# Top-k attention with a gated MLP on one core: the candidate search in five strided segments instead of six contiguous ones

## The chip, the cores and the metric

The kernel runs on one core of one Trainium2 chip. The metric is device time in microseconds for one launch. The engines that matter are TensorE (PE), VectorE (DVE), ScalarE (ACT) and GpSimd (POOL); each works through its own list of instructions in order, and they meet only through semaphores. DMA transfers are issued here from SyncE's queue (SP), and for some weights from POOL.

## The reference

There are 8 batches of 8 heads, 576 positions and a head size of 64. For every query the 32 largest of its 576 scores are kept, the rest are masked out, and a softmax over the kept ones weights the values. The result goes through a two-layer network with a leaky ReLU.

```python
scores = scale * np.matmul(q, k.transpose(0, 1, 3, 2))
kth = np.partition(scores, -top_k, axis=-1)[..., -top_k:-top_k + 1]   # top_k = 32
scores = np.where(scores >= kth, scores, -1000000000.0)
scores = scores - np.max(scores, axis=-1, keepdims=True)
attn = np.exp(scores)
attn = attn / (np.sum(attn, axis=-1, keepdims=True) + 1e-09)
x = np.matmul(attn, v)               # then (8, 8, 576, 64) -> (4608, 512)
h = x @ w_in                         # 512 -> 2048
g = np.maximum(h, 0.0) + alpha * np.minimum(h, 0.0)
out = g @ w_out                      # 2048 -> 512
```

Only the 32nd largest score of each row has to be known: it is the threshold of the mask.

## The kernel before

Two heads make a pair, so there are 32 pairs. The rows of a pair are cut into nine tiles of 128 queries (four for each head, and a ninth that holds the last 64 queries of both). That makes 288 tiles of 128 rows by 576 scores, in the order of the list ORDER. A main loop runs over ticks n. In each tick the loop issues, by hand-written order, one stage of several tiles on each engine: scores on PE for tile n + 1, the shift and sign on ACT for tile n, the selection on DVE for tiles n − 1 to n − 7, and in what is left, matmuls of the network for batches that are finished. The lags are LAG_S = 2 for the segment search, LAG_M = 3 for the merge and LAG_W = 7 for the mask. A calendar (put and run) places the preparation of later pairs and the products with the values at fixed ticks. Nothing reorders this list later.

How the threshold of a row is found:

- From the mean and the second moment of the row's scores, the prep steps (dve_2 to dve_6, L271 to L288) make a guess: mean + 1.6 standard deviations. It is subtracted in act_b (L337), so that b is positive for scores above the guess.
- act_s (L343) takes the sign of b and sums it, which gives the number of scores above the guess. side_of (L353, POOL) turns it into SG, which says whether the 32nd score lies above or below the guess.
- flip (L359, DVE) maps b to y by bit operations, so that the largest values of y are those nearest to the guess on the wanted side. The wanted score is then the r-th largest of y, where r follows from the count.
- seg_ops (L369, DVE) cuts the 576 values of y into segments and takes the eight largest of each with one MAX8 instruction per segment. They go into C, NSEG × 8 candidates per row.
- merge_ops (L384, L386, DVE) takes the 24 largest of the candidates in order: MAX8, then MATCH_REPLACE8, which blanks the eight just found (the profile shows a small MATCH_VALUE_LOAD ahead of it), twice over, then a third MAX8. The result is L.
- sel_eq, sel_pr and sel_sum (L397 to L407) pick the r-th of the 24 for three tiles at once, limit (L413) maps it back, mask (L433) compares b with it, and POOL multiplies the mask with the exponentials (L443). A DMA transpose brings the weights to PE for the product with the values (L494).

A segment could hold more than eight of the wanted scores. So check_group (L461) keeps the largest eighth candidate of each row's segments, and checks (L473, L474) compares it with the selected value at the end. If any row of any tile fails, final_flag (L482) sets a flag and the program goes on into general_batch, which computes everything again in a slower way.

On DVE, a tick issues the mask of one tile first, then the segment searches of another and the merge steps of a third one in turn, and then flip:

```python
for i in range(max(len(segs), len(merges), 2)):
    if i < len(segs):
        segs[i]()
    if i < len(merges):
        merges[i]()
```

So with six searches and five merge steps, one search stands behind each merge step. y has two buffers, C has two, one for each group of nine tiles, and C2, the merge's scratch, has one.

## Time and profile before

| what | value |
|---|---|
| time, median of 3 runs | 873.02 us (872.99 to 875.49) |
| the profiled execution: its own time | 873.98 us |
| the profiled execution: its span | 872.1 us |
| DVE busy | 835.1 us, 96% of the span |
| ACT busy | 790.3 us, 91% |
| PE busy | 721.9 us, 83% |
| POOL busy | 431.0 us, 49% |
| segment searches (L369, MAX8) | 1728, mean 243 ns |
| merge MAX8 (L384) | 864, mean 188 ns |

The span runs from the first to the last instruction in the profile; the execution's own time has a little more around it. A row of the groups names the line, the engine, the operation, the output and input tiles with their shapes (partitions × elements), the number of instances, the busy time and the mean duration in ns, and behind the last bar the idle time of the engine just ahead of these instructions, with what ended it. Durations of neighbours on one engine can overlap, so that the sum of durations may exceed the busy time. A row of stages gives for each stretch of time the busy us and the number of instructions of each engine, the clock granted to TensorE, the busy share of DMA and its GB/s.

### The profile page before, as it was taken

The page shows a single profiled execution, that of the slowest core. Times are in us where ns is not written, and L with a number is a line of the kernel's source. Part 1 is how long each engine was busy: PE and PEld are TensorE (multiplying, and loading weights), DVE is VectorE, ACT ScalarE, POOL GpSimd, SP SyncE. Part 2 cuts the span into 40 slices and gives each one's busy share as a digit, 9 for nine tenths or more (in the row PEclk, how much of TensorE's full clock was granted, in tenths as well). Part 3 has the DMA queues.
Part 4 walks back from the last instruction along what each step waited for, and adds up shares of the span by engine and source line. Part 5 has one row for each costly group of instructions (what it writes and reads, how often), then busy time and mean ns, then how long its engine had stood idle before and what let it go on. Part 6 is the DMA issues. An engine that isn't in the chain of part 4 may idle for free.

```text
span 872.1 us, 20608 instructions
## 1 busy us (share of the span) xinstructions
PE 721.9 (83%) x5697; PEld 428.3 (49%) x5771; DVE 835.1 (96%) x5188; ACT 790.3 (91%) x1873; POOL 431.0 (49%) x630
## 2 busy tenths in 40 slices
PE   6776688778978789787987789977897988899996
PEld 4443444334554345444454445643455554566674
DVE  4999999999999999999999999999999999999992
ACT  6999999999999999889999999989999899979861
POOL 1455545555454555545555455554554555544530
PEclk9997779899979999989998999989999999999999
DMA  7999644644665545564576445475455543535442
GB/s 161 156 178 199 131 89 90 126 91 97 135 139 107 108 102 116 100 135 95 114 154 115 98 97 116 111 136 98 92 128 121 121 103 81 106 71 100 91 96 56
DMA packets 342619, 99.37 MB, mean 114 GB/s; under 512 B 334672, under 2 KB 334944, under 8 KB 342496
## 3 DMA queue, kind: packets, MB, share of 16 engines
q1 hardware_dynamic: 340144, 95.58, 54.4%
q0 software_dynamic: 1152, 2.10, 2.0%
q8 instruction: 47, 0.77, 0.4%
q14 instruction: 76, 0.62, 0.2%
q10 hardware_dynamic: 1200, 0.30, 0.2%
HBM read 36.71 MB, written 9.44 MB: 53 GB/s over the span
## 4 chain that ended last, share of the span: by engine, by line
DVE 62%; ACT 21%; PE 12%; DMA 2%; issue 1%; POOL 1%; SPq 0%; DVEq 0%; another core or an unknown queue 0%; ACTq 0%
DVE C L369 20%; DVE y L359 9%; DVE mk L433 9%; DVE C L386 8%; DVE L L384 7%; ACT b L337 5%; ACT h L343 5%; ACT e L348 4%; PE ps L328 4%; PE pz L715 3%; PE ph L697 2%; ACT gT L703 2%; DVE P L246 2%; ACT xb L523 2%; PE pu L494 1%
## 5 line engine op out<-in xcount | busy, mean ns | idle before, releaser
L443 POOL TENSOR_TENSOR w<-mk,e 128x576 bf16<-128x576 bf16 x250 | 319.3, 1277 | 337.9 <-DVE mk L433 187.5
L369 DVE MAX8 C<-y 128x8 f32<-128x96 f32 x1728 | 419.1, 243 | 0.1
L328 PE MATMUL ps<-qkT 64*128 64x288 f32 (+1 forms) x1280 | 256.5, 474 | 35.1 <-ACT b L337 34.6
L337 ACT ACTIVATE b<-ps,NT 128x576 f32<-128x576 f32 x288 | 202.3, 761 | 3.1 <-PE ps L328 3.1
L343 ACT ACTIVATE h<-b 128x576 bf16<-128x576 f32 x288 | 202.9, 705 | 1.7
L697 PE MATMUL ph<-xT,w_in_b 128*128 128x128 bf16 (+2 forms) x997 | 150.4, 292 | 40.8 <-ACT gT L703 33.6
L328 PEld LDWEIGHTS ps<-qkT 64*128 64x128 f32 (+1 forms) x1280 | 134.3, 194 | 97.6 <-ACT b L337 59.8
L348 ACT ACTIVATE e<-b 128x1152 bf16<-128x1152 f32 (+1 forms) x158 | 174.2, 1102 | 0.0
L384 DVE MAX8 L<-C 128x8 f32<-128x48 f32 x864 | 162.6, 188 | 0.1
L359 DVE TENSOR_SCALAR y<-b,SG 128x576 int32<-128x576 int32 x288 | 147.0, 510 | 8.2 <-POOL SG L353 7.8
L433 DVE TENSOR_SCALAR mk<-b,KP 128x576 bf16<-128x576 f32 x282 | 143.6, 509 | 0.0
L715 PE MATMUL pz<-w_out_b,gT 128*128 128x512 bf16 x543 | 132.4, 380 | 1.2 <-issue 0.5
L697 PEld LDWEIGHTS <-w_in_b 128*128 128x128 bf16 x1024 | 80.4, 100 | 104.0 <-issue 79.6
L703 ACT ACTIVATE gT<-ph 128x512 bf16<-128x512 f32 x140 | 86.0, 621 | 28.1 <-PE ph L697 28.1
L386 DVE MATCH_REPLACE8 C<-L,C 128x48 f32<-128x48 f32 x576 | 108.3, 188 | 0.0
L715 PEld LDWEIGHTS <-gT 128*128 128x128 bf16 x560 | 51.6, 98 | 68.5 <-issue 14.0
L494 PE MATMUL pu<-v_bf,wT 128*128 128x65 bf16 (+1 forms) x1600 | 69.4, 198 | 14.4 <-DMA wT<-w 6.9
L494 PEld LDWEIGHTS <-wT 128*128 128x128 bf16 (+1 forms) x1600 | 65.2, 103 | 25.6 <-issue 10.2
L353 POOL TENSOR_SCALAR SG<-S_all 128x1 int32<-128x1 f32 x288 | 65.3, 227 | 18.9 <-ACT h L343 18.8
L443 POOL TENSOR_TENSOR wm<-mk,e 128x576 bf16<-128x576 bf16 x32 | 40.8, 1276 | 49.9 <-DVE mk L433 45.6
L343 ACT ACTIVATION_READ_ACCUMULATOR h<-b 128x1 f32 x288 | 62.8, 218 | 0.0
L523 ACT ACTIVATE xb<-pu,rz 128x64 bf16<-128x64 f32 x224 | 54.5, 369 | 0.0
(113 smaller groups left out, 728.1 us busy)
## 6 DMA issues: line engine op xcount, KB each, us to landing
out_dram<-o_sb SPq DMA_DIRECT2D x34, 256.0 KB, 2.3
st_q<-in_q_dram SPq DMA_DIRECT2D x64, 128.0 KB, 2.8
st_v<-in_v_dram SPq DMA_DIRECT2D x64, 128.0 KB, 2.6
kst<-in_k_dram SPq DMA_DIRECT2D x62, 128.0 KB, 2.6
w_stage<-in_moe_w_out_dram SPq DMA_DIRECT2D x16, 256.0 KB, 3.1
w_in_b<-in_moe_w_in_dram POOLq DMA_DIRECT2D x8, 256.0 KB, 6.4
wT<-w SPq DMA_TRANSPOSE x128, 3.3
st_q<-in_q_dram SPq DMA_DIRECT2D x32, 32.0 KB, 2.5
```

The lines of the kernel that those rows point to most:

```text
L328: nc.tensor.matmul(o_, l_, r_, start=True, stop=True)
L337: nc.scalar.activation(t["b"].rearrange("p (a c) -> p a c", a=2), t["ps"], AF.Identity, bias=NT0[:, p * TPP + j:p * TPP + j + 1], scale=ON ...
L343: nc.scalar.activation(h, tiles[n]["b"], AF.Sign, accum_out=S_all[:, n:n + 1])
L348: nc.scalar.activation(e, tiles[n0]["bu"], AF.Exp, scale=scl)
L359: nc.vector.tensor_scalar(t["y"].bitcast(I32), t["b"].bitcast(I32), FLIP, SG[:, n:n + 1], ALU.bitwise_xor, ALU.bitwise_xor)
L369: return [lambda g=g: nc.vector.max(out=C[:, n % TPP, g, :], in_=t["y"][:, g * SEG:(g + 1) * SEG]) for g in range(NSEG)]
L384: ops.append(lambda r=r, src=src: nc.vector.max(out=L[:, 8 * r:8 * r + 8], in_=src))
L386: ops.append(lambda r=r, src=src: nc.vector.match_replace(out=C2, in_to_replace=L[:, 8 * r:8 * r + 8], in_values=src, imm_value=NEG))
L433: nc.vector.tensor_scalar(t["mk"], t["b"], row_limit(n), None, ALU.is_ge)
L443: nc.gpsimd.tensor_tensor(dst, t["mk"], t["e"], ALU.mult)
L697: nc.tensor.matmul(hold[f][:, i, :], w_in_b[:, kk, (f + i) * 128:(f + i + 1) * 128], xT[:, kk, c0:c0 + tb], start=(kk == 0), stop=(kk == N ...
L715: nc.tensor.matmul(pz[0:m], hold["gT"][:, f, r0:r0 + m], w_out_b[:, f, :], start=False, stop=(f == NFT - 1))
```

## The change

The 576 values of y are cut into five segments instead of six. A segment is no longer a block of 96 neighbours but every fifth value: segment g holds the values g, g + 5, g + 10 and so on, 116 of them for g = 0 and 115 for the others. y is fp32, so two values of a segment lie 20 bytes apart. As NSEG also sets the shapes of C and C2, a row has 40 candidates instead of 48, which the three MAX8 and two MATCH_REPLACE8 of the merge read, and the group's check reads five eighths of each row instead of six. The number of merge instructions stays.

```diff
 S = 576
-NSEG = 6
-SEG = S // NSEG
+NSEG = 5
 KW = 24
...
         C = Cs[n // TPP]
         t = tiles[n]
-        return [lambda g=g: nc.vector.max(out=C[:, n % TPP, g, :],
-                                          in_=t["y"][:, g * SEG:(g + 1) * SEG])
+        return [lambda g=g: nc.vector.max(out=C[:, n % TPP, g, :], in_=t["y"][:, g:S:NSEG])
                 for g in range(NSEG)]
```

## The prediction

> **What bounds the kernel now.** First the busy table of the profile page, then the busy time by stage, because a share over the span says nothing of where it lies.

> ```profile
> span 872.1 us, 20608 instructions
> PE 721.9 (83%) x5697; PEld 428.3 (49%) x5771; DVE 835.1 (96%) x5188; ACT 790.3 (91%) x1873; POOL 431.0 (49%) x630
> ```

> ```profile
> core 0: us, PE busy (x) PEld busy (x) DVE busy (x) ACT busy (x) POOL busy (x), PEclk, DMA share, GB/s
> 40.00:100.00 60.00, 42.61 (x273) 26.19 (x277) 58.72 (x367) 59.46 (x135) 33.61 (x48) 0.84 0.96 179
> 200.00:300.00 100.00, 82.98 (x607) 46.82 (x616) 100.00 (x631) 95.19 (x237) 52.23 (x74) 0.93 0.57 117
> 500.00:600.00 100.00, 84.46 (x684) 49.31 (x697) 100.00 (x626) 93.61 (x227) 52.49 (x74) 0.97 0.56 113
> 760.00:800.00 40.00, 37.15 (x298) 24.60 (x301) 37.15 (x224) 33.56 (x72) 20.27 (x30) 0.92 0.48 92
> 860.00:872.10 12.10, 5.40 (x59) 4.68 (x56) 0.42 (x1) 2.44 (x5) 0.00 (x0) 0.86 0.09 28
> ```

> In the two long middle stages DVE is busy 100.00 of 100 us. It never waits there, so whatever is added to its instruction stream is added to the time one for one. ACT follows at 94 to 95%: a shorter DVE stream would run into ACT soon, a longer one has nothing to hide behind. What DVE waits for outside these stages is in the list of its waits; it is all that could absorb added work:

> ```profile
> DVE y L359 <- POOL SG L353: 7.8, 6, 3.5
> DVE o_sb L606 <- DMA out_dram<-o_sb: 6.5, 1, 6.5
> DVE P L246 <- PE pr L238: 2.7, 3, 1.9
> DVE sq L271 <- ACT M L267: 1.6, 2, 1.0
> ```

> The wait at L606 is in the tail, behind the last tile, and stays. The other three sum to 12.1 us; they are waits of the tile pipeline on ACT or PE, which have room when DVE takes longer. Part of them falls before the pipeline is full, so I let 5 us be absorbed.

> **What a tile costs on DVE.** The groups by line and shape, DVE alone:

> ```profile
> L369 DVE MAX8 C<-y 128x8 f32<-128x96 f32 x1728 | 419.1, 243 | 0.1
> L384 DVE MAX8 L<-C 128x8 f32<-128x48 f32 x864 | 162.6, 188 | 0.1
> L386 DVE MATCH_REPLACE8 C<-L,C 128x48 f32<-128x48 f32 x576 | 108.3, 188 | 0.0
> L246 DVE TENSOR_TENSOR P<-pr,qkT 128x512 bf16<-128x512 f32 x32 | 21.9, 684 | 2.8 <-PE pr L238 2.7
> L407 DVE TENSOR_REDUCE KK<-L 128x3 f32<-128x72 f32 x96 | 20.7, 216 | 0.1
> L461 DVE TENSOR_REDUCE M<-C 128x9 f32<-128x54 f32 x32 | 7.5, 235 | 0.0
> L246 DVE TENSOR_TENSOR P<-pr,qkT 128x64 bf16<-128x64 f32 x32 | 6.8, 212 | 0.0
> L281 DVE TENSOR_TENSOR t<-sq,t 128x9 f32<-128x9 f32 x32 | 5.1, 159 | 0.1
> L284 DVE TENSOR_REDUCE sq<-t 128x9 f32<-128x27 f32 x32 | 5.0, 157 | 0.1
> L271 DVE TENSOR_TENSOR sq<-M,sq 128x9 f32<-128x9 f32 x32 | 4.7, 146 | 1.6 <-ACT M L267 1.6
> ```

> These durations overlap: the next instruction starts before the one in front has ended. The timeline of one tick (start, duration) shows by how much:

> ```profile
> 403.53 0.25 DVE L369 MAX8 C<-y 128x8 f32<-128x96 f32 x1
> 403.70 0.19 DVE L384 MAX8 L<-C 128x8 f32<-128x48 f32 x1
> 403.81 0.24 DVE L369 MAX8 C<-y 128x8 f32<-128x96 f32 x1
> 403.97 0.07 DVE L386 MATCH_VALUE_LOAD C<-L,C 128x8 f32 x1
> 404.03 0.19 DVE L386 MATCH_REPLACE8 C<-L,C 128x48 f32<-128x48 f32 x1
> 404.14 0.25 DVE L369 MAX8 C<-y 128x8 f32<-128x96 f32 x1
> ...
> 405.02 0.24 DVE L369 MAX8 C<-y 128x8 f32<-128x96 f32 x1
> 405.20 0.52 DVE L359 TENSOR_SCALAR y<-b,SG 128x576 int32<-128x576 int32 x1
> ```

> A search of 0.24 to 0.25 us holds the engine for 0.16 to 0.18 us, one over 48 elements (0.19) for 0.11: about 78 ns less than the duration in each case. So the path price of an instruction is its duration less 78 ns: 243 − 78 = 165 ns for a search today, 990 ns for the six of a tile.

> **The change part by part.**

> *One search fewer, each longer, read with a step of five.* Five searches cover 116, 115, 115, 115, 115 scores, 115.2 on average, and each score lies 20 bytes behind the one before it. If they lay side by side, the price would follow from three rows on one line: 48 elements 188 ns, 72 elements 216 ns (L407), 96 elements 243 ns, that is 133 ns + 1.146 ns per element. But no long step-of-five read is in the trace. The nearest row is the reduce at L461: it reads the eighth of each eight candidates, so 54 single fp32 values, 32 bytes apart. With the fixed 133 ns it pays (235 − 133) / 54 = 1.89 ns per element, against 1.146 side by side. Its nine short rows are not the reason: L284 also has nine rows, of three neighbours, and takes 157 ns for 27 elements, 126 ns + 27 × 1.146.

> The ends: with L284's 126 ns as the fixed part the reduce pays (235 − 126) / 54 = 2.02 ns. With the slope of the two L246 forms, (684 − 212) / 448 = 1.05 ns, the reduce at L407 has 216 − 72 × 1.05 = 140 ns fixed, and L461 pays (235 − 140) / 54 = 1.76 ns; the search's own fixed part is then 243 − 96 × 1.05 = 142 ns. I take 1.89 since it rests on the rows that are fitted by one line, the search among them. A search then lasts 133 + 115.2 × 1.89 = 351 ns and holds DVE for 273; five hold it 1365 ns. That is +375 ns per tile. By the low end it is 142 + 115.2 × 1.76 = 345, held 267, five 1335: +345. By the high end 133 + 115.2 × 2.02 = 366, held 288, five 1440: +450.

> [...]

> *The merge over 40 candidates.* Three MAX8 and two MATCH_REPLACE8 lose eight elements each: 5 × 8 × 1.146 = −46 ns per tile (−42 at 1.05). The two 8-value loads stay.

> *The order.* Searches and merge steps are issued in turn, six and five of them; after, five and five. A search still stands between each merge step and the one that needs its result; the last merge MAX8 now stands last, and flip or the selection follows, which don't read it directly in most ticks. Cost zero, covered by the search in between, which becomes longer. If that cover went, a merge step would wait out the 78 ns overlap, 4 × 78 ns × 288 = 90 us, but there is no reason that it goes.

> *The group's check* reads 45 values instead of 54, 32 times: 9 × 1.89 × 32 = −0.5 us. No DMA, wait or instruction of another engine moves; the tiles C and C2 shrink.

> *The sum.* Per tile 375 − 46 = +329 ns, times 288 tiles +94.8 us; less 0.5, less 5 absorbed: +89. By the ends (345 − 42) × 288 − 5.5 = +82 and (450 − 46) × 288 − 5.5 = +111. The profiled execution took 873.98 us, 1.9 more than its span, and the median of the runs is 873.02, 1.0 below it. So 872.1 + 89 + 1.9 − 1.0 = **962 us**, between 955 and 984 by the ends. As a step of 20 bytes isn't one of 32, I widen to prices of 1.64 and 2.12 ns: 0.25 ns lower is 115.2 × 0.25 × 5 × 288 = 41 us, 0.23 higher 38 us, so 921 to 1000.

> **The rivals.**

> *The step costs nothing (faster).* A search lasts 133 + 115.2 × 1.146 = 265 ns, held 187, five 935: 935 − 990 − 46 = −101 ns per tile, −29 us of DVE work. ACT at 95% of a steady stage would stand at 98%, so a few us are lost to it: about 848 us. It decides below the point where five searches cost 990 + 46 = 1036 ns, 207 each, or (285 − 133) / 115.2 = 1.32 ns per element. Speaking for it: a search may have slack per element that a fetch hides in. Against: the plain MAX8 already follows the same line as the reduce of L407, so neither has slack, and L461 lies above by 0.74 ns per element. Chance 0.06; another 0.02 that it ends within 0.3%, about what a measurement of this kernel can tell from no change.

> *A short step costs more than that of L461.* L281 reads one operand and writes its result in steps of 12 bytes, and takes 159 ns against 146 for the plain L271: 13 / 9 = 1.4 ns more per element, 2.5 in all, though with two strided streams and on only nine elements. At 2.5 ns: 133 + 288 = 421, held 343, five 1715: (1715 − 1036) × 288 − 5.5 = +190, so 1063 us. Chance 0.09. A mild price, 1.36 to 1.6 ns, gives 878 to 914 us: chance 0.04.

> *The change doesn't do what it says: the general path runs.* The flag at L482 sends the whole batch through general_batch if in any of 36,864 rows the selected value is below the eighth candidate of a segment. Larger segments make that likelier. In a count over the reference's inputs, with the threshold formula of the prep steps in fp32 and bf16, ranks from 1 to 18 below the guess are wanted, and no segment of every fifth score holds more than 7 of a row's wanted ones; eight with the wanted value elsewhere would be needed. Rounding on the chip can shift a rank by one. If it ran: 320 tiles of 128 rows with seven passes over 576 elements, 7 × (133 − 78 + 576 × 1.146) ns = 5.0 us each, 1.6 ms on top, 2.5 ms or more. Chance 0.03.

> **How the numbers follow.** The forecast, prices of 1.6 to 2.12 ns, has 0.76. Slower by over 0.3%: 0.76 + 0.09 + 0.04 + 0.03 = 0.92; same 0.02; faster 0.06. The range 920 to 1000 holds nearly all of the 0.76 and a little of the mild case; the free step and the steep one lie outside.

> **What would show it.** In the profile of the changed kernel L368 (the search, one line up) has 1440 instances over 116 or 115 elements at about 351 ns; MAX8 and MATCH_REPLACE8 over 40 at 179 ns; the middle stages have DVE at 100 of 100 us and ACT near 86; the wait of y on SG shrinks. A search at 265 ns would make the step free; a search at 421 the steep case; DVE below 98% in the middle would mean that something else bounds. A span of milliseconds is the general path.

## The result, and the profile after

The changed kernel takes 960.68 us (median of 5 runs, 960.52 to 961.57) against 873.06 us for the kernel before: a ratio of 1.0995, 95% interval 1.0982 to 1.1009. It is 10% slower. The forecast was 962 us.

The page of the changed kernel begins with these lines (busy us, share of the span, instructions):

```profile
span 958.8 us, 20320 instructions
PE 752.7 (79%) x5697; PEld 443.2 (46%) x5771; DVE 930.0 (97%) x4900; ACT 796.7 (83%) x1873; POOL 430.2 (45%) x630
...
DVE 96%; PE 1%; ACT 1%; DMA 1%; SPq 0%; issue 0%; POOL 0%; DVEq 0%; ACTq 0%
```

DVE has 288 instructions fewer and is busy 94.9 us longer (835.1 to 930.0). The span grew by 86.7 us. The last line is the chain of work that ended last, followed back through what released each step: it is now DVE for 96% of the span. On the page of the kernel before the same line is:

```profile
DVE 62%; ACT 21%; PE 12%; DMA 2%; issue 1%; POOL 1%; SPq 0%; DVEq 0%; another core or an unknown queue 0%; ACTq 0%
```

This chain leaves DVE at every release, however short the wait, so the 62% alone do not say how much DVE waited before; that is measured below. The groups of DVE by shape show which instructions grew:

```profile
L368 DVE MAX8 C<-y 128x8 f32<-128x115 f32 x1152 | 395.6, 344 | 0.0
L382 DVE MAX8 L<-C 128x8 f32<-128x40 f32 x864 | 149.6, 173 | 0.1
...
L368 DVE MAX8 C<-y 128x8 f32<-128x116 f32 x288 | 101.2, 351 | 0.1
L384 DVE MATCH_REPLACE8 C<-L,C 128x40 f32<-128x40 f32 x576 | 99.6, 173 | 0.0
```

The timeline of the changed kernel (start, duration) gives what a search holds the engine for, from one start to the next:

```profile
405.20 0.34 DVE L368 MAX8 C<-y 128x8 f32<-128x115 f32 x1
405.47 0.06 DVE L384 MATCH_VALUE_LOAD C<-L,C 128x8 f32 x1
405.53 0.17 DVE L384 MATCH_REPLACE8 C<-L,C 128x40 f32<-128x40 f32 x1
405.63 0.34 DVE L368 MAX8 C<-y 128x8 f32<-128x115 f32 x1
405.90 0.17 DVE L382 MAX8 L<-C 128x8 f32<-128x40 f32 x1
406.00 0.34 DVE L368 MAX8 C<-y 128x8 f32<-128x115 f32 x1
```

A search of 0.34 us holds DVE for 0.27, a merge step over 40 for 0.10. Over all instances in the trace the mean from start to start is 272 ns for 115 elements and 280 for 116. Per tile that is 4 × 272 + 280 = 1368 ns where six searches took 6 × 164 = 984.

The stages, and the list of DVE's waits:

```profile
200.00:300.00 100.00, 77.91 (x553) 43.38 (x560) 100.00 (x526) 84.08 (x202) 46.61 (x67) 0.86 0.54 110
...
500.00:600.00 100.00, 80.55 (x598) 45.29 (x605) 100.00 (x529) 84.88 (x209) 46.28 (x65) 0.88 0.49 96
```

```profile
DVE y L358 <- POOL SG L352: 4.8, 2, 3.2
...
DVE sq L270 <- ACT M L266: 1.0, 1, 1.0
DVE P L245 <- PE pr L237: 0.5, 1, 0.5
```

DVE stays at 100 of 100 us in the middle; ACT falls from 94 to 95% to 84 to 85%.

### The profile page after: what moved, and what is told of

It reads as the page before. It is cut to its first block, busy times and chain, and to the rows that moved or that the text cites. A ratio compares the mean times of both kernels' runs of the same rounds, so it can differ in the third digit from the quotient of the medians.

```text
span 958.8 us, 20320 instructions
## 1 busy us (share of the span) xinstructions
PE 752.7 (79%) x5697; PEld 443.2 (46%) x5771; DVE 930.0 (97%) x4900; ACT 796.7 (83%) x1873; POOL 430.2 (45%) x630
## 4 chain that ended last, share of the span: by engine, by line
DVE 96%; PE 1%; ACT 1%; DMA 1%; SPq 0%; issue 0%; POOL 0%; DVEq 0%; ACTq 0%
DVE C L368 40%; DVE y L358 13%; DVE mk L431 13%; DVE C L384 10%; DVE L L382 9%; DVE P L245 2%; DVE L L401 1%; DVE KK L405 1%; DVE EQ L395 1%; DVE KP L411 1%; DVE M L459 0%; PE ph L581 0%; DVE t L277 0%; PE pz L601 0%; DMA kst<-in_k_dram 0%
## 5 line engine op out<-in xcount | busy, mean ns | idle before, releaser
L368 DVE MAX8 C<-y 128x8 f32<-128x115 f32 (+1 forms) x1440 | 496.7, 345 | 0.1
L327 PE MATMUL ps<-qkT 64*128 64x288 f32 (+1 forms) x1280 | 261.7, 485 | 47.0 <-ACT b L336 46.3
L695 PE MATMUL ph<-xT,w_in_b 128*128 128x128 bf16 (+2 forms) x997 | 161.0, 307 | 30.8 <-ACT gT L701 21.0
L382 DVE MAX8 L<-C 128x8 f32<-128x40 f32 x864 | 149.6, 173 | 0.1
L358 DVE TENSOR_SCALAR y<-b,SG 128x576 int32<-128x576 int32 x288 | 144.0, 500 | 4.8 <-POOL SG L352 4.8
L695 PEld LDWEIGHTS <-w_in_b 128*128 128x128 bf16 x1024 | 84.2, 105 | 100.9 <-issue 72.7
L492 PE MATMUL pu<-v_bf,wT 128*128 128x65 bf16 (+1 forms) x1600 | 76.6, 207 | 68.1 <-DVE P L245 54.0
L492 PEld LDWEIGHTS <-wT 128*128 128x128 bf16 (+1 forms) x1600 | 71.7, 110 | 82.8 <-issue 64.7
L384 DVE MATCH_REPLACE8 C<-L,C 128x40 f32<-128x40 f32 x576 | 99.6, 173 | 0.0
```

The lines of the kernel that those rows point to most:

```text
L327: nc.tensor.matmul(o_, l_, r_, start=True, stop=True)
L358: nc.vector.tensor_scalar(t["y"].bitcast(I32), t["b"].bitcast(I32), FLIP, SG[:, n:n + 1], ALU.bitwise_xor, ALU.bitwise_xor)
L368: return [lambda g=g: nc.vector.max(out=C[:, n % TPP, g, :], in_=t["y"][:, g:S:NSEG]) for g in range(NSEG)]
L382: ops.append(lambda r=r, src=src: nc.vector.max(out=L[:, 8 * r:8 * r + 8], in_=src))
L384: ops.append(lambda r=r, src=src: nc.vector.match_replace(out=C2, in_to_replace=L[:, 8 * r:8 * r + 8], in_values=src, imm_value=NEG))
L695: nc.tensor.matmul(hold[f][:, i, :], w_in_b[:, kk, (f + i) * 128:(f + i + 1) * 128], xT[:, kk, c0:c0 + tb], start=(kk == 0), stop=(kk == N ...
```

## The experiments

The theory was that the cost lies in the read: each score lies alone, and DVE pays about 0.74 ns more for each. The rivals were the length of a search, each hop of the address, and contention inside the kernel. A second question came up on the way: how much a search without this penalty would gain.

**Pairs of neighbours in place of single scores.** This keeps five segments and 40 candidates.

```diff
-        return [lambda g=g: nc.vector.max(out=C[:, n % TPP, g, :], in_=t["y"][:, g:S:NSEG])
+        return [lambda g=g: nc.vector.max(out=C[:, n % TPP, g, :], in_=t["y"].rearrange("p (u w) -> p u w", w=2)[:, g:S // 2:NSEG, :])
                 for g in range(NSEG)]
```

> Five segments as in the change, but each takes every fifth pair of neighbouring scores (58 or 57 pairs, two words side by side, then a hop of 40 bytes) in place of every fifth score. Theory (what costs is that each element lies alone): a search costs as a contiguous one, held about 187 ns against the 272 between starts after the change; 5 x 187 - 6 x 164 - 45 = -94 ns per tile of DVE work, -27 us, and with ACT at 98% a few us lost: 848 us, between 843 and 858. Rival A (each hop costs, however long the run): half as many hops, 57 x 0.74 x 5 = +211 ns per tile on top, about 900 us. Rival B (the longer search costs more, the step nothing): 961 us as after the change.

Measured: 869.68 us, ratio to before 0.9952 (0.9935 to 0.997). The groups of DVE:

```profile
L368 DVE MAX8 C<-y 128x8 f32<-128x116 f32 x864 | 229.1, 265 | 0.1
...
L368 DVE MAX8 C<-y 128x8 f32<-128x114 f32 x576 | 150.4, 261 | 0.0
```

A search of 116 scores in pairs takes 265 ns, as the line of the contiguous rows gives it (133 + 116 × 1.146 = 266). So neither the length nor the hop costs: the penalty is gone with pairs. But the time is not the expected 848 us. About 22 of the 27 us that DVE was to save did not come through; this is followed up below.

**Five segments of neighbours.** The count of the change without its step.

```diff
+CUT = (0, 120, 234, 348, 462, 576)
...
-        return [lambda g=g: nc.vector.max(out=C[:, n % TPP, g, :], in_=t["y"][:, g:S:NSEG])
+        return [lambda g=g: nc.vector.max(out=C[:, n % TPP, g, :], in_=t["y"][:, CUT[g]:CUT[g + 1]])
```

> Five segments of neighbours, 120 scores in the first and 114 in the other four: the count of the change without its step. Theory: search held about 187 ns, 848 us, as with the pairs. Rival B (length): 961 us.

Measured: 870.93 us, ratio 0.9971 (0.9952 to 0.9991). The searches of 114 take 261 ns, as in the run with pairs. Pairs cost what neighbours cost, and again the time missed 848 us.

**Six segments of every sixth score.** The step without the count.

```diff
-NSEG = 5
+NSEG = 6
```

> Six segments of every sixth score, 96 each: the step without the change of count, with 48 candidates as before. Theory: a search has 96 elements at about 0.75 ns more each, held 164 + 72 = 236 ns; 6 x 72 x 288 = +124 us, some 8 absorbed: 989 us. Rival B (length): 873 us, as before.

Measured: 987.08 us, ratio 1.1303 (1.1273 to 1.1334). A search over the same 96 elements goes from 243 to 311 ns:

```profile
L368 DVE MAX8 C<-y 128x8 f32<-128x96 f32 x1728 | 537.1, 311 | 0.1
```

The expectation of 989 us is met. The step alone costs 113 us (the kernel before took 874.11 beside it); the smaller count takes back 26 of them (987 to 961). The length is ruled out as the cause.

**The step by itself, first probe.** Behind the end of the changed kernel, over a scratch tile X, 16 MAX8 (or reduces) of each shape stand back to back:

```diff
+        for i in range(16):
+            nc.vector.max(out=Z[:, 4, i, :], in_=X[:, 0:575:5])
...
+        for i in range(16):
+            nc.vector.max(out=Z[:, 11, i, :], in_=po[:, 0:290:5, :])
```

> The changed kernel, with 16 MAX8 of each of 14 shapes, and 16 reduces of two, back to back on DVE behind its end, over a scratch tile, when the other engines have nearly ended. Time between starts for 115 elements. Theory by the reduce of the trace before: contiguous about 187 ns; every step from 2 words on about 270; pairs of 58 about 187. Rival C (lines of 16 bytes, two elements of a line in a row at full rate): step 2 about 187, steps of 4 and more about 270, step 3 between. Rival D (contention with GpSimd inside the kernel): step 5 is well below 270 here. By the 2.5 ns of the steep rival, step 24 words gives about 343. The reduce over 115 shows the same difference between step 1 and step 5 as MAX8, if it lies in the read.

The timeline of the probe, 16 instances a row (start, and length of the whole group). From top to bottom: steps of 1, 2, 3, 4, 5, 6, 8, 16 and 24 words; 48 elements at step 5; 58 pairs from an even word, from an odd word, 29 fours, each with a step of five groups; 48 neighbours; then the reduce at steps 1 and 5:

```profile
954.60 2.96 DVE L936 MAX8 Z<-X 128x8 f32<-128x115 f32 x16
957.47 2.95 DVE L938 MAX8 Z<-X 128x8 f32<-128x115 f32 x16
960.34 3.44 DVE L940 MAX8 Z<-X 128x8 f32<-128x115 f32 x16
963.69 4.25 DVE L942 MAX8 Z<-X 128x8 f32<-128x115 f32 x16
967.85 4.30 DVE L944 MAX8 Z<-X 128x8 f32<-128x115 f32 x16
972.06 4.23 DVE L946 MAX8 Z<-X 128x8 f32<-128x115 f32 x16
976.20 4.32 DVE L948 MAX8 Z<-X 128x8 f32<-128x115 f32 x16
980.42 4.10 DVE L950 MAX8 Z<-X 128x8 f32<-128x115 f32 x16
984.42 5.59 DVE L952 MAX8 Z<-X 128x8 f32<-128x115 f32 x16
989.93 2.39 DVE L954 MAX8 Z<-X 128x8 f32<-128x48 f32 x16
992.25 2.96 DVE L956 MAX8 Z<-X 128x8 f32<-128x116 f32 x16
995.13 3.54 DVE L958 MAX8 Z<-X 128x8 f32<-128x116 f32 x16
998.58 2.97 DVE L960 MAX8 Z<-X 128x8 f32<-128x116 f32 x16
1001.47 1.83 DVE L962 MAX8 Z<-X 128x8 f32<-128x48 f32 x16
1003.22 2.94 DVE L964 TENSOR_REDUCE Z<-X 128x1 f32<-128x115 f32 x16
1006.08 4.29 DVE L967 TENSOR_REDUCE Z<-X 128x1 f32<-128x115 f32 x16
```

The distance of two rows over 16 is the time between starts. Neighbours take (957.47 − 954.60) / 16 = 179 ns, and a step of two words takes the same 179. A step of three takes 209, of four 260, of five 263, of eight 264, of 24 words 344. So an element that lies alone is not what costs: with a step of two each lies alone, and nothing is lost. That part of the theory falls, and rival C, lines of 16 bytes, fits: a step of two leaves two elements in each line, a step of four one. Contention is ruled out as a large part: 263 ns here against 272 in the kernel. The trace of the changed kernel says the same: searches of 115 that run wholly beside an instruction of POOL hold DVE for 273 ns (567 of them), those without one for 275 (106). The reduce has 179 and, by the length of its group, 263 as well, so the price lies in the read, not in MAX8.

**Lines of 16 bytes, second probe.** The same with other shapes.

```diff
+        X8 = X.rearrange("p (u w) -> p u w", w=8)
...
+            nc.vector.max(out=Z[:, 5, i, :], in_=X8[:, 0:58, 3:5])
...
+            nc.vector.max(out=Z[:, 6, i, :], in_=X8[:, 0:58, 0:3:2])
```

> The changed kernel with 16 MAX8 of each of 15 shapes over 116 elements behind its end, in this order: contiguous; step 2 from word 0; step 2 from word 1; 58 pairs, one in each 32 bytes, at words 0-1, 1-2, 3-4, then words 0 and 2, 0 and 4; single elements at steps of 5, 8, 12, 24, 32, 40, 48 words. Theory now (what costs is that an element is the only one taken from its 16 bytes, words 0 to 3 of an aligned four): contiguous, both steps of 2, and pairs at 0-1, 1-2 and 0 and 2 about 180 ns between starts; pairs at 3-4 and at 0 and 4, and steps of 5, 8, 12 about 263. Rival (words must be neighbours in 8 aligned bytes): 1-2 and 0 and 2 about 263. For the long steps: 24 words 344 as seen; if this goes by the step's size 32 to 48 are as much, if by a bank some are back at 263.

The rows of the pairs at words 1-2, at 3-4, at 0 and 2, at 0 and 4, and the one behind them for its start:

```profile
968.26 2.97 DVE L942 MAX8 Z<-X 128x8 f32<-128x116 f32 x16
971.14 4.28 DVE L944 MAX8 Z<-X 128x8 f32<-128x116 f32 x16
975.34 2.98 DVE L946 MAX8 Z<-X 128x8 f32<-128x116 f32 x16
978.22 4.28 DVE L948 MAX8 Z<-X 128x8 f32<-128x116 f32 x16
982.41 4.36 DVE L950 MAX8 Z<-X 128x8 f32<-128x116 f32 x16
```

Words 1-2 take 180 ns and so do words 0 and 2, which are no neighbours. Words 3-4, which are neighbours but lie in two aligned fours (counted from the start of the row), take 262, as do 0 and 4. With words 1-2 and 0 and 2 at 180 ns the rival of neighbours in 8 aligned bytes falls, which had 263 for them. In these two probes, then, an element cost more where it was the only one that the instruction took from its aligned 16 bytes before it went on: 250 to 267 ns for 115 or 116 elements, all alone, at steps of 4 to 16 words and in the pairs at 3-4 and at 0 and 4, against 179 to 181 ns where two or four came from each. This reading is rough where lone elements and pairs alternate: at a step of three half of the elements are alone, which would give 221 ns, and the first probe has 209. For the long steps the same view gave 346 ns at 24 words, 253 at 32, 283 at 40 and 253 at 48: the extra at 24 does not grow with the step, and what sets it stays open.

**Where the gain of a free read goes.** Five searches without the penalty leave DVE about 100 ns less per tile (between tiles 48 and 240, summed from start to start, searches and merge take 1653 ns before and 1566 with pairs, and 16 of these are waits), but a tile takes 2.82 us in place of 2.87, half of that. A wait is counted here, and below, where the distance to the next start is over 15 ns above the median of the same instruction. First the question whether DVE bounds at all any more:

```diff
-NSEG = 5
+NSEG = 4
```

on top of the pairs, so that DVE has yet less to do.

> The full kernel with four segments of every fourth pair, 144 scores each, 32 candidates: per tile 4 searches of about 216 ns in place of 5 of 186, and a merge over 32: some 100 ns less DVE work again. Theory (ACT with its waits on PE is the bound once DVE has less to do): no more than 3 us below the five segments of pairs, 866 to 870 us. Rival (DVE still bounds): 28 us below, about 842. If a row had more candidates in one segment than the eight kept, the general path would run, and the time would be milliseconds.

Measured: 869.27 us (0.9926 to 0.9965 of before), within half a microsecond of the run with five, as the theory had it. But the trace shows that this is no test of it, since DVE did not get less to do: searches and merge take 1586 ns per tile, 20 more than with five. Four searches cannot stand between five merge steps, and the last two merge steps follow each other directly:

```profile
406.31 0.17 DVE L384 MATCH_REPLACE8 C<-L,C 128x32 f32<-128x32 f32 x1
406.40 0.29 DVE L368 MAX8 C<-y 128x8 f32<-128x144 f32 x1
...
406.98 0.17 DVE L384 MATCH_REPLACE8 C<-L,C 128x32 f32<-128x32 f32 x1
407.19 0.20 DVE L382 MAX8 L<-C 128x8 f32<-128x32 f32 x1
```

With a search behind it a MATCH_REPLACE8 takes 93 ns to the next start, with the MAX8 that reads its result right behind it 211 (189 of each). This is the cover whose loss the prediction priced at 78 ns; here it costs 118.

What holds the five segments of pairs is better read from their own trace. Its stages:

```profile
200.00:300.00 100.00, 83.78 (x638) 46.36 (x639) 99.76 (x606) 96.62 (x240) 52.80 (x75) 0.95 0.59 118
...
500.00:600.00 100.00, 85.56 (x702) 49.24 (x702) 99.75 (x604) 96.19 (x234) 53.81 (x77) 0.98 0.59 115
```

DVE's 99.75 us look as full as before, but the busy share does not show waits that are shorter than the overlap of durations (78 ns for a search before, some 80 for a mask): by the starts DVE waits 50 ns per tile, 23 at P for PE, 22 at y for SG, where before the change it was 3. ACT stands at 95 to 97%. What it waits for between 160 and 700 us is almost only PE's results of the network, which stand in ACT's order:

```profile
ACT gT L701 <- PE ph L695: 14.6, 16, 2.6
ACT o_sb L718 <- PE pz L713: 9.1, 6, 1.6
```

With its 514.8 us of work that fills 538.5 of the 540 us, and in the same stretch PE's waits name ACT alone. So the next pair of runs leaves most of the network out, without and with pairs:

```diff
-        for f in range(0, NFT, fpp):
-            yield (lambda f=f: ph_step(f)), (lambda f=f: ph_act(f)), 0.9, 1
...
-            for i in range(part * 7, min(part * 7 + 7, NKT + NFT)):
+            for i in range(NKT):
```

> The kernel before with the hidden layer of the network left out in all blocks but the last 128 rows (only x times the folded identity weights is written): ACT loses most of its ReLU reads, PE most of its network matmuls. DVE has the same work of six contiguous searches per tile. Theory (before, DVE and ACT stand close, and DVE sets the pace): nearly the time before less the end of the network, about 835 to 865 us; DVE stays at 100% in the middle, ACT drops to about 85%. It is the base for the next run.

> The same left out, with five segments of pairs. Theory (the 27 us that pairs save on DVE were lost in the full kernel because ACT, with its waits for PE's network results, can't go faster than some 2.8 us a tile): with ACT relieved the saving comes through, 96 ns x 288 = 28 us less than the run without pairs, between 22 and 30. Rival (the pairs save DVE time that is lost again on DVE or at its waits on POOL): some 5 us less, as in the full kernel.

Measured: 871.99 us with six contiguous segments, 855.86 with pairs. The first was above the range expected: DVE's work is the same and sets the time alone (0.9982 of before, 0.9966 to 0.9999), and the end does not shrink. So in the kernel before, the network's work on ACT and PE was no bound; in both traces DVE waits 3 ns per tile. With pairs 16 us of the 28 come through, three to four times what the full kernel gave, and still not all. The rest showed in the timelines of POOL and DVE. These are one tick of the full kernel with pairs, POOL first:

```profile
406.02 1.27 POOL L441 TENSOR_TENSOR w<-mk,e 128x576 bf16<-128x576 bf16 x1 [1.29 <-DVE mk L431]
407.27 0.22 POOL L352 TENSOR_SCALAR SG<-S_all 128x1 int32<-128x1 f32 x1
```

```profile
405.43 0.51 DVE L431 TENSOR_SCALAR mk<-b,KP 128x576 bf16<-128x576 f32 x1
...
407.61 0.51 DVE L358 TENSOR_SCALAR y<-b,SG 128x576 int32<-128x576 int32 x1
408.04 0.51 DVE L431 TENSOR_SCALAR mk<-b,KP 128x576 bf16<-128x576 f32 x1
```

The mask mk lets POOL start w, SG stands behind w in POOL's queue, y waits for SG, and the next mask stands behind y. From mask to y this takes at least 2.09 us in the traces with this order. The delay, 22 ns per tile at y, stands in no row of DVE's waits between 160 and 700 us, since it is shorter than the overlap of durations, some 80 ns for a mask or a y (0.51 us long, 0.43 to the next start). In the run with pairs, y begins within 0.15 us of SG's end in 145 of 191 ticks (78 of 187 before, none after the change). One way out is to issue the short SG first:

```diff
+            if 0 <= n - 1 < NT:
+                side_of(n - 1)
             due = wdue.get(n, ())
...
-            if 0 <= n - 1 < NT:
-                side_of(n - 1)
```

> The full kernel with five segments of pairs, and the sign SG of the next tile (a 0.23 us step) put on POOL ahead of the weight product w (1.27 us) of the same tick in place of behind it. In the traces so far DVE's y follows the end of SG within 0.15 us in 145 of 191 ticks of the run with pairs, in 78 of 187 before, in none after the change: mask on DVE, w and SG on POOL, then y on DVE is a ring that takes at least 2.09 us from mask to y. Theory (this ring ate a part of the 96 ns that pairs save): y no longer waits for w, and up to 48 ns x 288 = 14 us more come through, 855 to 866 us, less what ACT then holds. Rival (ACT with its waits on PE alone is the bound): unchanged at 868 to 871.

> The kernel with pairs and without the hidden layer (all blocks but the last 128 rows), with SG first as well. There ACT has room, and the ring on POOL should be all that held the saving to 16 us of 28. Theory: 28 us below the run without the hidden layer and with six segments, 840 to 848 us. Rival: 856 as with SG behind w.

> The full kernel with four segments of pairs and SG first. DVE has some 100 ns per tile less than with five. If the ring alone was the bound, some 25 us below the run with five and SG first; if ACT is the next bound (2.69 us of work per tile and its waits on PE), no more than 5 us below it. I expect the second.

> The kernel before, six contiguous segments, with SG first. Its DVE is at 100% in the middle, and mask to y takes 2.09 us at the least by its own instructions too. Theory: DVE is the bound by itself, 869 to 874 us, at most 4 us below before. If it falls by 10 us or more, DVE waited for the ring in the kernel before too, hidden behind the overlap of its instructions.

Measured: the full kernel with pairs and SG first 867.53 us (0.9919 to 0.9964 of before), above the range expected and no clear difference to pairs alone at 869.68; without the network 847.05, 25 us below the 871.99 of six contiguous segments; four segments with SG first 871.42, not below the run with five but 3.9 us above, and again with the last merge steps uncovered; the kernel before with SG first 874.28 (0.9984 to 1.0026 of before). So without the network the ring held back 8 to 9 us (855.86 to 847.05), and with it gone 25 of the 28 us expected come through: in that run's trace DVE waits for nothing between tiles 48 and 240.

In the full kernel SG first does not take POOL out of DVE's way. By the starts DVE still waits 57 ns per tile, 16 at P for PE and 34 in twelve ticks where y, or EQ ahead of it, begins while w is still running. One of them, POOL first:

```profile
410.38 1.28 POOL L441 TENSOR_TENSOR w<-mk,e 128x576 bf16<-128x576 bf16 x1
```

```profile
410.75 1.00 DVE L395 TENSOR_TENSOR EQ<-ra,iota 128x72 f32<-128x72 f32 x1
411.67 0.51 DVE L358 TENSOR_SCALAR y<-b,SG 128x576 int32<-128x576 int32 x1
```

EQ, else 0.2 us long, lasts until 0.09 us after w's end. In this trace the seven EQ that begin more than 0.2 us ahead of w's end take 0.78 to 1.00 us and end 0.09 to 0.10 us after it, and the five y that do so take 0.59 to 0.82 us and end 0.31 to 0.32 us after it, though no result passes between the two. So DVE and POOL do not meet only through semaphores here; by what else they meet, the runs don't show. Searches run beside POOL unharmed: 0.26 us beside w, 0.26 to 0.27 without, in the same trace. In all twelve ticks w stands right behind an SG for which POOL had been idle, for 2.19 to 4.19 us, until ACT's sign h, so it was ACT that made w late. On this reading the full kernel is held by ACT or PE with the network's work; leaving the network out relieved both at once, so which of the two it is stays open.

The fastest of all are full kernels with pairs, 0.3 to 0.6% below the kernel before; five segments of neighbours give 0.3%. The change's count is of some use, its step is not.

## Why the prediction was right

*DVE is the bound and pays one for one.* Right, though the reason given, 100 of 100 us busy, is not enough: with pairs DVE is at 99.75 and is not the bound. It is shown by the starts, where DVE waits 3 ns per tile before and none after (tiles 48 to 240), and by the run without the network, where 871.99 us remain when ACT and PE have less to do. 94.9 us more busy time gave 86.7 us more span.

*The search.* 351 ns of duration and 273 of held time were forecast; 344 to 351 (345 on the mean) and 272 to 280 (274) were measured: a duration 6 ns too long and an overlap 6 ns too wide cancelled. The row at L461 was the right one to read, and that its nine rows were not the reason is shown by the reduce of the first probe, one row, 179 and 263 ns, and by its own distance to the next start, 160 ns, where the probe's prices below give 59 + 54 × 1.77 = 155. The two parts of the price were each a little off and made up for each other: by the probe, contiguous elements cost (179.4 − 109.4) / 67 = 1.04 ns, not 1.146, and single ones (263 − 59) / 115 = 1.77, not 1.89, with some 9 ns more for a search inside the kernel. What costs is narrower than "a step": a step of two words was free in the probe (179 ns against 179). That a row with a step of 32 bytes could stand for one of 20 was not known beforehand; neither takes two elements from one aligned 16 bytes, and in the probe they cost the same (264 and 263 ns).

*The merge* was to give 46 ns per tile and gave 25 + 17 = 42 (three MAX8, two MATCH_REPLACE8, from start to start); the order's cost of zero held, since the last merge step holds DVE for the same 0.10 us.

*What is absorbed* was mis-sized: 5 us forecast, 8.2 measured (DVE's idle time went from 37.0 to 28.8 us). The waits of y, P and sq gave 3.0, 2.2 and 0.6, and those for PE's products with the values 2.4. The last are not in the prediction's list of waits, which leaves out rz (3.2 and 1.1 us before), km (3.4) and xT (1.3).

*The sum*: +94.8 − 0.5 on DVE against +94.9 measured; 962 us against 960.68.

*The rivals.* The general path did not run. A price of 2.5 ns was measured, but at a step of 24 words (344 ns, (344 − 59) / 115 = 2.48), not of five. The faster rival had the wrong time: with the step's cost gone, 848 us was forecast and 870 measured. The step that failed is the sentence that ACT would stand at 98% with a few us lost to it. ACT, with its waits on PE in its order, stayed at 95 to 97%, and half of what DVE saved per tile came back as its waits for PE and for SG. So for a change that takes work off DVE this kernel had 3 to 5 us to give, not 29, and the break-even price of 1.32 ns holds for DVE's work alone.

## What to carry to other kernels

On a bound VectorE, look at how many elements an instruction takes from each aligned 16 bytes: one fp32 from each cost about 0.73 ns more for each element here (263 ns against 179 for 115 elements), two from each cost nothing (179 and 180 ns). Here the scattered selection could be made in pairs, which loses the penalty, and the general path still did not run. An added cost on the engine that binds could be summed from the rows of the trace; a saving on it could not, as another engine stood at 95% with waits of its own: the same arithmetic that gave +89 us to 2 us gave −25 where −4 came. Whether an engine binds is better read from the distances between starts than from its busy share, 100 in the one case and 99.75 in the other.
